# A fused FFT, feed-forward and expert kernel: plain float32 forward products for the first batch, steps moved from GpSimd to VectorE, and another order at the opening, the join and the last block

## The chip, the cores and the metric

The kernel runs on one core of one Trainium2 chip. The metric is the device time of one execution in microseconds (us), taken as the median of several runs. The engines are TensorE (PE in the profile, with its weight loads as PEld), VectorE (DVE), ScalarE (ACT), GpSimd (POOL) and SyncE (SP, which issues most of the transfers).

## The reference

Three stages follow one another over 8 batches of 3072 tokens with 256 channels (24,576 tokens). All that matters of it:

```python
y = irfft(rfft(x, axis=1) * (filt_r + 1j * filt_i), n=3072, axis=1)
h = y @ w_in                                     # 256 -> 2048
y = where(h > 0, h, exp(min(h, 0)) - 1) @ w_out  # 2048 -> 256
e = argmax(y @ w_gate); p = softmax(y @ w_gate)[e]
out = p * sigmoid(y @ w_output_gate)[e] * (relu(y @ w1[e]) @ w2[e])   # 8 experts, 256 -> 1024 -> 256
```

`w_in` and `w_out` arrive as float64. All else is float32.

## The kernel before, in words

**Products.** A float32 value is split into a high part, which is a fast float32r number, and a low part; a product of two values is three float32r products (high by high, high by low, low by high). A table that is known beforehand comes already split from memory.

**The Fourier stage.** One batch has two halves of 128 channels, and a unit of work is one half. A unit first runs butterflies on VectorE (`f1`, `f2`, lines 174 to 196 with the helper of line 167). Then six pairs of frequency groups follow, each with these steps: `hi` (ACT, line 235) and `lo` (DVE, line 239) split the input, `neg` (ACT, line 245) makes the negative, `fwd` multiplies by the forward table on PE (length 128, line 264: six float32r products of 128x256 for a group; the two real groups use plain float32, line 260), `mul` and `add` (DVE, lines 281 to 294) apply the filter, `yhi` and `ylo` (lines 299, 303) split again, `inv` (PE, lines 317 and 318) multiplies by the inverse table, and `evac` (ACT, line 332) empties PSUM. Backward butterflies in parts called `q0`, `q1`, `q2` and so on (lines 377 to 416, 465 to 470) produce `y`.

**The opening.** Before the list of slots starts, both units of batch 0 run in one stream (`us[0]`, `us[1]`). Their filter and table tiles lie in room that the weights use later (`own`). Two of the second unit's first butterflies (lines 174, 175) run on GpSimd (`pool=(0, 1)`). Into the same stream go the first steps of `Wide`, which turns a quarter of the float64 weights into float32 halves: `load`, `scale` (ACT), `bits` and `value` (DVE, lines 557, 558, 561), `high` (ACT, line 564) and `low` (GpSimd, line 568), and for `w_out` also `turn` and `gate_w` (lines 948 to 960), which multiply by the gate weights. The framework's scheduler orders the opening on each engine. It ends with the first 512 tokens' `ys`, split on ACT (line 1111) and DVE (line 1113).

**Slots.** Everything up to the end of the feed-forward stage is a list of slots. Slot (c, m) is one sixteenth of a chunk of 512 tokens: `mm1` (six products of 128x512, line 685), the elu (ACT lines 689 and 690, DVE line 691), the split of the result (line 697 on ACT, 698 on DVE), and, three slots later, `mm2` (twelve products of 128x264, line 708). There are 48 chunks, so 768 slots. `at(slot, fn, pe)` hangs further steps on a slot, `level` spreads a list of DVE steps over a stretch of slots by a table of load (`LOAD`, n/960 + 0.155 for a step of n columns), `plan_unit` lays a Fourier unit of a later batch over the slots from `t0` with `GAP` slots between pairs, and `plan_rest` places what the opening leaves over: the other quarters of the weights, the rest of batch 0's backward steps (`q2` on GpSimd), and small loads. Within a slot the order on every engine is the order of the code.

**The join and the expert stage.** While the last chunks run, the tokens are sorted by expert (`rank`, `scatter`). Two early blocks of 256 tokens (numbers -2 and -1) are computed at the seam: `transposes` (line 1286), `up2` (48 products, line 1334) and `down` (48 products, line 1349), then the table of blocks is read and `blocks(0, 98)` runs over the others; a block's rows come by `load_rows` (line 1278), and `put` (line 1363, GpSimd) scatters each half of its output, as two halves `q`. A block takes the transposes of the next one between its own `up2` and `down`. Behind the blocks stands a test of how many more there are (the load is at line 1447); here the branch isn't taken.

Of the kernel before, what the change touches and what calls it, by code (L numbers as in the profile page):

```python
# [56 lines left out]
def dft_tables():  # L57
# [7 lines left out]
    fwd, inv = [], []  # L65
    for a, b in PAIRS:
        for g in (a, b):
            kap = KAPPA[g]
            if kap is None:
# [6 lines left out]
                fwd.append(np.concatenate([ca, cb, sa, sb], 1).astype(np.float32))  # L76
                rr, ii = np.zeros((W, 2 * W)), np.zeros((W, 2 * W))
# [5 lines left out]
            else:  # L83
# [7 lines left out]
    return np.concatenate(fwd, 1).astype(np.float32), np.concatenate(inv, 1).astype(np.float32)  # L91
# [3 lines left out]
class Fft:  # L95
# [35 lines left out]
    def unit(self, b, h, own=None):  # L131
# [397 lines left out]
class Wide:  # L529
# [9 lines left out]
    def steps(self, src, place, place_c, dst):  # L539
# [34 lines left out]
def fft_moe_kernel(ctx, tc, x, filt_r, filt_i, w_in, w_out, wg, wog, w1, w2, out):  # L574
# [3 lines left out]
    fwd_np, inv_np = dft_tables()  # L578
# [901 lines left out]
```

## Time and profile before

| what | us |
|---|---|
| runs shown | 3808.22, 3808.24, 3805.9 |
| median | 3808.22 |
| the profiled execution's own time | 3805.89 |
| its span in the profile | 3804.1 |
| PE busy in the span | 3700.6 (97%) |
| DVE / ACT / POOL busy | 2537.9 / 2067.4 / 625.6 |
| granted clock of PE over the span | 0.990 |

The span is what the profile shows of the execution; the profiled execution's time lies 1.8 us above it and 2.3 us below the median. The span falls into four parts: the opening up to the first slot at 118.4 us, the slots up to about 2600 us, the join up to about 2634 us, and the blocks up to 3789 us. The granted clock is a share of full speed, 2.4 GHz; 0.5 is 1.2 GHz.

### The profile page before, as it was taken

The numbers are of one execution on the slowest core, as the hardware profiler recorded it, in microseconds if no ns is written. First come the engines' busy times: TensorE is split into PE (matmuls) and PEld (weight loads), VectorE is DVE, ScalarE is ACT, GpSimd is POOL, SyncE is SP. The second block draws the span as 40 slices with busy tenths as digits, with TensorE's granted clock in tenths as the row PEclk, the third lists the DMA queues.
The fourth block names the chain that finished last, engine by engine and source line by source line (L and its number), as shares of the span: only waits on it lengthen the run. The fifth ranks groups of instructions, "written<-read, shape, count | busy, mean of one in ns | idle before, by whom it ended". The sixth has DMA issues, their size and how long they took to land. (4 is left out here: it accounts for less than half of the span.)

```text
span 3804.1 us, 70253 instructions
## 1 busy us (share of the span) xinstructions
PE 3700.6 (97%) x26364; PEld 3481.6 (92%) x26364; DVE 2537.9 (67%) x5210; ACT 2067.4 (54%) x3897; POOL 625.6 (16%) x730
## 2 busy tenths in 40 slices
PE   4799999999999999999999999999999999999998
PEld 4689899999999999999999999999999999999998
DVE  8889888888888788788887875554333333333333
ACT  3466666666666666666666666664333333333332
POOL 1311111111111111111111111111111111111111
PEclk9799999999999999999999999999999999999999
DMA  7354434343353442533425232201212121222221
GB/s 220 120 161 142 131 124 138 103 157 111 106 158 111 133 127 86 172 114 124 137 96 160 95 109 70 91 18 41 90 47 93 46 91 46 91 91 69 68 91 38
DMA packets 235411, 400.83 MB, mean 105 GB/s; under 512 B 21554, under 2 KB 154298, under 8 KB 228922
## 3 DMA queue, kind: packets, MB, share of 16 engines
q1 hardware_dynamic: 216250, 344.68, 29.1%
q0 software_dynamic: 18816, 51.60, 3.7%
q8 instruction: 210, 3.44, 0.4%
q14 instruction: 135, 1.11, 0.1%
HBM read 674.76 MB, written 115.04 MB: 208 GB/s over the span
## 5 line engine op out<-in xcount | busy, mean ns | idle before, releaser
L708 PEld LDWEIGHTS z<-wex,g 128*128 128x128 f32 x9216 | 1229.4, 189 | 71.0 <-DVE rt L726 3.4
L708 PE MATMUL z<-wex,g 128*128 128x264 f32 x9216 | 1251.4, 285 | 3.0 <-DVE rt L726 3.0
L685 PE MATMUL h<-ys,win 128*128 128x512 f32 x4608 | 1206.6, 397 | 23.0 <-DVE e L691 11.4
L685 PEld LDWEIGHTS h<-ys,win 128*128 128x128 f32 x4608 | 818.0, 189 | 163.5 <-DVE e L691 14.3
L691 DVE SCALAR_TENSOR_TENSOR e<-e,h 128x512 f32<-128x512 f32 x768 | 525.7, 685 | 477.7 <-ACT e L690 469.5
L689 ACT ACTIVATE e<-h 128x512 f32<-128x512 f32 x768 | 459.4, 598 | 682.3 <-PE h L685 670.6
L1334 PE MATMUL h<-zt,w1s 128*128 128x256 f32 x4800 | 592.1, 283 | 1.0 <-ACT zt L1288 0.7
L1334 PEld LDWEIGHTS h<-zt,w1s 128*128 128x128 f32 x4800 | 581.9, 191 | 1.9 <-ACT zt L1288 0.9
L1349 PE MATMUL o<-w2s,hs 128*128 128x256 f32 x4704 | 573.6, 281 | 0.0
L1349 PEld LDWEIGHTS o<-w2s,hs 128*128 128x128 f32 x4704 | 556.1, 188 | 0.1
L698 DVE TENSOR_TENSOR g<-e,g 128x512 fp32r<-128x512 f32 x768 | 548.1, 714 | 0.1
L690 ACT ACTIVATE e<-e 128x512 f32<-128x512 f32 x768 | 485.8, 633 | 24.5
L1340 DVE SCALAR_TENSOR_TENSOR hs<-h,hs 128x512 fp32r<-128x512 f32 x392 | 271.2, 692 | 306.1 <-ACT hs L1339 302.4
L697 ACT CAST g<-e 128x512 fp32r<-128x512 f32 x768 | 464.3, 605 | 6.7 <-DVE e L691 6.7
L1339 ACT ACTIVATE hs<-h 128x512 fp32r<-128x512 f32 x392 | 234.1, 597 | 330.9 <-PE h L1334 329.2
L1363 POOL DMA_INDIRECT out_dram<-o,rows x196 | 192.8, 984 | 964.7 <-ACT o L1356 547.5
L779 POOL DMA_INDIRECT rows_d<-rt,sl x192 | 206.7, 1076 | 779.6 <-DVE sl L775 345.2
L1356 ACT ACTIVATE o<-o,ogv 128x256 f32<-128x256 f32 x196 | 82.2, 470 | 452.6 <-PE o L1349 452.6
L1300 DVE TENSOR_SCALAR ogv<-ogv 128x2 f32<-128x2 f32 x98 | 16.6, 169 | 376.0 <-ACT ogv L1299 376.0
L756 POOL TENSOR_TENSOR A<-A,ohb 128x8 bf16<-128x8 bf16 x192 | 69.1, 360 | 911.7 <-DVE rt L747 846.3
L803 POOL TENSOR_TENSOR ps<-pw,ps 128x512 fp32r<-128x512 f32 x64 | 88.2, 1378 | 365.4 <-ACT ps L798 347.4
L317 PE MATMUL pf<-ci,YH 128*128 128x256 f32 x528 | 129.9, 282 | 1.5 <-ACT YH L299 1.5
(288 smaller groups left out, 2882.8 us busy)
## 6 DMA issues: line engine op xcount, KB each, us to landing
w1s<-wpk SPq DMA_DIRECT2D x198, 1024.0 KB
w2s<-wpk SPq DMA_DIRECT2D x198, 1024.0 KB
ci<-dft_inv SPq DMA_DIRECT2D x73, 768.0 KB
cf<-dft_fwd SPq DMA_DIRECT2D x87, 512.0 KB
wpk<-ps SPq DMA_DIRECT2D x64, 512.0 KB
rows<-rows_d SPq DMA_DIRECT2D x98, 258.0 KB
y<-yd SPq DMA_DIRECT2D x46, 512.0 KB
fl<-fs SPq DMA_DIRECT2D x84, 256.0 KB
```

The lines of the kernel that those rows point to most:

```text
L685: nc.tensor.matmul(out=ps, lhsT=win_s(m // 4)[:, a, k, m % 4 * W:m % 4 * W + W], rhs=s[:, q, k], start=(n == 0), stop=(n == 5))
L689: nc.scalar.activation(out=e, in_=ps, func=AF.Relu, scale=-1.0)
L690: nc.scalar.activation(out=e, in_=e, func=AF.Exp, scale=-1.0)
L691: v.scalar_tensor_tensor(out=e, in0=e, scalar=-1.0, in1=ps, op0=ALU.add, op1=ALU.max)
L697: nc.scalar.copy(out=s[:, 0], in_=e)
L698: v.tensor_tensor(out=s[:, 1], in0=e, in1=s[:, 0].bitcast(F32), op=ALU.subtract)
L708: nc.tensor.matmul(out=Z[c][i], lhsT=s[:, q, i * W:i * W + W], rhs=wex_s(m // 4)[:, a, m % 4], start=(m == 0 and q == 0 and a == 0), stop= ...
L779: g.indirect_dma_start(out=rows_d, out_offset=bass.IndirectOffsetOnAxis(ap=f["sl"][:, i:i + 1], axis=0), in_=f["rt"][:, i, NE:NE + ROW], i ...
L1334: nc.tensor.matmul(out=ps[:, q * TB:q * TB + TB], lhsT=w1s(mp // 2)[:, a, k, m * W:m * W + W], rhs=s[:, z, k], start=(n == 0), stop=(n == 5))
L1339: nc.scalar.activation(out=hi, in_=p2, func=AF.Relu)
L1340: v.scalar_tensor_tensor(out=lo, in0=p2, scalar=0.0, in1=hi.bitcast(F32), op0=ALU.max, op1=ALU.subtract)
L1349: nc.tensor.matmul(out=pss[q], lhsT=hs(z, k // 2)[:, k % 2, q * W:q * W + W], rhs=w2s(k // 4)[:, a, k % 4], start=(k == 0 and n == 0), sto ...
```

## The change

1. **Forward products of batch 0.** The groups of length 128 are multiplied as two plain float32 products (of 128x256) by an unsplit table (`plain`, 512 or 768 columns in place of 1024). `lo` does nothing there and `neg` covers one half of what it did.
2. **From GpSimd to VectorE.** `low` of `Wide` (eight in all), the two first butterflies of the second unit, and the `q2` steps of batch 0 run on VectorE.
3. **Less ahead of the first slot.** Of the second quarter of `w_in` and the second of `w_out`, only `scale` and a load stand there; the first quarter of `w_out` is converted between the two halves' last steps (up to `gate_w`), its remaining steps behind them. `low` of a quarter of `w_out` is a step of its own behind the second `gate_w`.
4. **Slots.** `plan_rest` has another table with its loads counted; the two units of batch 1 start at slots 30 and 58 in place of 20 and 56, the first with three slots between pairs in place of four; the load of its input moves from slot 8 to 13.
5. **Join.** The transposes of the two early blocks go four and three slots ahead of where `up2(-2)` starts (before: three ahead, and two behind). The rows of block 0 are loaded ahead of the weights; its transposes stand inside `down(-1)`, behind 36 of its 48 products. The load for the later test moves ahead of the blocks.
6. **Last block.** `down` computes all of output half 0, then all of half 1.

The core of the diff:

```diff
+                plain.append(fwd[-1])
...
+                plain.append(np.concatenate([c, s], 1).astype(np.float32))
...
-            H = P[i]["H"] = st.tile([W, 2, 2, 3, W], F32R, tag="H", name="H", bufs=2)
+            H = P[i]["H"] = st.tile([W, 2, 2, 3, W], F32 if own else F32R, tag="H", name="H", bufs=2)
             for dst, src in halves(i, H):
                 nc.scalar.copy(out=dst[:, 0], in_=src)
...
         def lo(i):
+            if own:
+                return
...
-                nc.scalar.activation(out=H[:, :, j, 2], in_=H[:, :, j, 0].bitcast(F32), func=AF.Copy, scale=-1.0)
+                parts = slice(0, 1) if own else slice(0, 2)
+                nc.scalar.activation(out=H[:, parts, j, 2], in_=H[:, parts, j, 0].bitcast(F32), func=AF.Copy, scale=-1.0)
...
-                cc = p["c"][:, 512 * j:512 * j + 512]
+                cc = p["c"][:, 256 * j:] if own else p["c"][:, 512 * j:512 * j + 512]
...
+                if own:
+                    for m in range(2):
+                        nc.tensor.matmul(out=o, lhsT=cc[:, m * W:m * W + W],
+                                         rhs=p["H"][:, 0, j, m:m + 2].rearrange("p c d -> p (c d)"), start=(m == 0), stop=(m == 1))
...
         def low():
             hi, lo = dst()
-            nc.gpsimd.tensor_tensor(out=lo, in0=T["c"], in1=hi.bitcast(F32), op=ALU.subtract)
+            v.tensor_tensor(out=lo, in0=T["c"], in1=hi.bitcast(F32), op=ALU.subtract)
...
-            LOAD[t] = {2: 0.85, 3: 1.65, 6: 1.4, 12: 0.7, 13: 0.7}.get(t % 16, 0.0)
+            LOAD[t] = {14: 0.7, 15: 0.7}.get(t, 0.0) if t < 16 else {2: 0.85, 3: 1.65, 6: 1.4, 12: 0.7, 13: 0.7}.get(t % 16, 0.0)
...
-    GAP = 4
-
-    def plan_unit(b, h, t0, prev, nxt, early=False):
+
+    def plan_unit(b, h, t0, GAP, prev, nxt, early=False):
...
-            level([(213, fn) for fn in p["q2"]] + [(1024, fn) for fn in p["y2"][:2]] + [(0, p["y2"][2])], t1 + 5, t1 + 16)
+            level([(213, fn) for fn in p["q2"]] + [(1024, fn) for fn in p["y2"][:2]] + [(0, p["y2"][2])], t1 + 5, t1 + 12)
...
-        return steps + [lambda: turn(0), lambda: gate_w(0), lambda: turn(1), lambda: (low(), gate_w(1))]
+        return steps + [lambda: turn(0), lambda: gate_w(0), lambda: turn(1), lambda: gate_w(1), low]
...
-        c = cf[i] = fft.st.tile([W, 1024], F32R, tag="cf", name="cf") if ORDER.index(i) % 2 else room("win1")[:, 0:1024]
-        nc.sync.dma_start(out=c.bitcast(F32), in_=fwd_d[:, 1024 * i:1024 * i + 1024])
+        c = fft.st.tile([W, 1024], F32, tag="cf", name="cf") if ORDER.index(i) % 2 else room("win1", F32)[:, 0:1024]
+        o, n = sum(768 if k == 2 else 512 for k in range(i)), 768 if i == 2 else 512
+        cf[i] = c[:, 0:n]
+        nc.sync.dma_start(out=cf[i], in_=plain_d[:, o:o + n])
...
-          fft.unit(0, 1, dict(own, AT=X00.rearrange("p a k d -> p (a k) d"), Z=Z1, T=Z1, pool=(0, 1)))]
-    parts = [u["parts"](nc.gpsimd) for u in us]
+          fft.unit(0, 1, dict(own, AT=X00.rearrange("p a k d -> p (a k) d"), Z=Z1, T=Z1, pool=()))]
+    parts = [u["parts"](v) for u in us]
...
-    for fn in wide_steps[1, 0][1:] + wide_steps[0, 1][1:] + wide_steps[1, 1][:1]:
+    for fn in (wide_steps[0, 1][1], wide_steps[1, 0][1]):
         fn()
...
+        if h == 0:
+            for fn in wide_steps[1, 0][2:8]:
+                fn()
...
+    for fn in wide_steps[1, 0][8:] + wide_steps[1, 1][:1]:
+        fn()
     Y[0] = ys0
-    U0 = 11
+    U0 = 18
...
+        for k, q, slots, tg in ((0, 1, (None, None, 0, 1, 2, 2), ()),
+                                (1, 1, (None, 2, 3, 3, 4, 5), (4, 5, 5, 6)),
+                                (0, 2, (3, 5, 6, 6, 7, 7), ()),
+                                (1, 2, (4, 6, 7, 7, 8, 9), (8, 9, 9, 10)),
+                                (0, 3, (7, 9, 10, 10, 11, 12), ()),
+                                (1, 3, (8, 10, 11, 11, 12, 13), (12, 13, 13, 14))):
+            st = wide_steps[k, q]
...
-    def down(j, then=lambda k: None):
+    def down(j, then=lambda k: None, last=False):
...
+        for k, q in [(k, q) for q in range(2) for k in range(8)] if last else [(k, q) for k in range(8) for q in range(2)]:
+            for n, (z, a) in enumerate(((0, 0), (0, 1), (1, 0))):
+                nc.tensor.matmul(out=pss[q], lhsT=hs(z, k // 2)[:, k % 2, q * W:q * W + W], rhs=w2s(k // 4)[:, a, k % 4],
+                                 start=(k == 0 and n == 0), stop=(k == 7 and n == 2))
+            if q:
+                then(k)
+            if k < 7:
+                continue
...
-            down(j, then=lambda k: load_w(j + 1, 1, k // 4) if more and k % 4 == 3 else None)
+            down(j, then=lambda k: load_w(j + 1, 1, k // 4) if more and k % 4 == 3 else None, last=not more)
...
+                t0 = (U0 + 12, U0 + 40)[h] if b == 1 else 96 * (b - 1) - 4 + 48 * h
+                gap = 3 if (b, h) == (1, 0) else 4
...
-                          (-3, lambda: transposes(-2), True), (-2, lambda: gates(-2), False),
+                          (-4, lambda: transposes(-2), True), (-3, lambda: transposes(-1), True), (-2, lambda: gates(-2), False),
                           (0, lambda: up2(-2, (0, 1)), True), (1, table_count, True), (1, lambda: up2(-2, (2, 3)), True),
-                          (2, lambda: transposes(-1), True), (2, lambda: down(-2), True),
+                          (2, lambda: down(-2), True),
...
+        es_m2.close()
+        es_m.close()
+        open_moe2()
+        load_rows(0)
...
+        def beside(k):
+            if k == 5:
+                transposes(0)
+            if k % 4 == 3:
+                load_w(0, 1, k // 4)
+
+        down(-1, then=beside)
...
+        some_more = nc.values_load(T2["nblk"], engines=[mybir.EngineType.SP, mybir.EngineType.PE, mybir.EngineType.DVE, mybir.EngineType.Activation, mybir.EngineType.Pool], min_val=0, max_val=NBLK, skip_runtime_bounds_check_because=why)
         blocks(0, NBLK - 3 - NEARLY)
-    some_more = nc.values_load(T2["nblk"], engines=[mybir.EngineType.SP, mybir.EngineType.PE, mybir.EngineType.DVE, mybir.EngineType.Activation, mybir.EngineType.Pool], min_val=0, max_val=NBLK, skip_runtime_bounds_check_because=why)
```

How the change moves instructions shows at three places. First, GpSimd's own list from its start (each row is a line, operation and names; the numbers in names only tell tiles apart). Before:

```order
L174 TENSOR_TENSOR Z<-win_120 128x1024
L175 TENSOR_TENSOR win_120<-win_120 128x1024
L568 TENSOR_TENSOR win_658<-win_120,win_658 128x1024
L568 TENSOR_TENSOR wex_811<-raw,wex_811 128x4x256
L568 TENSOR_TENSOR win_846<-raw,win_846 128x1024
L405 TENSOR_TENSOR Z_118<-Z_118 128x128
```

After (line 765 is the 754 of before, in the slots):

```order
L765 COPY A_1511<-acc_79 128x8
L767 ISA
L767 TENSOR_TENSOR A_1511<-A_1511,ohb 128x8 x4
L790 DMA rows_d<-rt,sl 196608x258 x2
L814 TENSOR_TENSOR ps<-pw,ps 128x512
```

The two butterflies, every `low` and the `q2` steps have left GpSimd's list.

Second, VectorE at the end of the opening, from the last steps of the last pairs on (`raw` is the weights' raw tile, `Z` the backward butterflies). Before:

```order
L303 TENSOR_TENSOR YH<-ab,YH 128x512
L557 TENSOR_SCALAR raw<-raw 128x1024
L303 TENSOR_TENSOR YH<-ab,YH 128x512
L558 SCALAR_TENSOR_TENSOR raw<-raw 128x1024
L557 TENSOR_SCALAR raw<-raw 128x1024
L561 SCALAR_TENSOR_TENSOR raw<-raw 128x1024
L558 SCALAR_TENSOR_TENSOR raw<-raw 128x1024
L377 TENSOR_TENSOR Z_118<-Z_118 128x768
L561 SCALAR_TENSOR_TENSOR raw<-raw 128x1024
L960 TENSOR_TENSOR wex_811<-pf,wex_811 128x2x8 x2
```

After:

```order
L313 TENSOR_TENSOR YH<-ab,YH 128x512
L415 TENSOR_TENSOR AA<-Z_118 128x128
L416 TENSOR_TENSOR AA<-Z_118 128x128
L567 TENSOR_SCALAR raw<-raw 128x1024
L313 TENSOR_TENSOR YH<-ab,YH 128x512
L568 SCALAR_TENSOR_TENSOR raw<-raw 128x1024
L387 TENSOR_TENSOR Z_118<-Z_118 128x768
L571 SCALAR_TENSOR_TENSOR raw<-raw 128x1024
```

Of two groups of three weight steps one is left there.

Third, PE at the join (`er` are the early blocks' rows, `zt` their transposed halves, `z` the last slots' `mm2`). Before, from the last `mm2` to `down(-2)`:

```order
L708 MATMUL z_28463<-wex_948,g 128x264
L708 MATMUL z_28465<-wex_948,g 128x264
L1334 MATMUL h_28898<-zt,w1s 128x256 x12
L1334 MATMUL h_28913<-zt,w1s 128x256 x12
...
L1334 MATMUL h_28941<-zt,w1s 128x256 x12
L1334 MATMUL h_28956<-zt,w1s 128x256 x12
L1286 MATMUL pf<-ct,er 128x128 x4
L1349 MATMUL o_28987<-w2s,eh 128x256 x3
```

After, from the slots ahead of it on:

```order
L1311 MATMUL pf<-ct,er 128x128 x4
L719 MATMUL z_28362<-wex_866,g 128x264 x2
L719 MATMUL z_28364<-wex_866,g 128x264 x2
...
L1311 MATMUL pf<-ct,er 128x128 x4
L719 MATMUL z_28362<-wex_866,g 128x264 x2
...
L1359 MATMUL h_28847<-zt,w1s 128x256 x12
L1359 MATMUL h_28862<-zt,w1s 128x256 x12
L1375 MATMUL o_28885<-w2s,eh 128x256 x3
```

Block -1's transposes have gone from between `up2(-2)` and `down(-2)` to between two slots' `mm2`.

## Rows read from the trace of the kernel before

**Rows 1.** The page, part 1: busy time of each engine over the whole span.
```profile
PE 3700.6 (97%) x26364; PEld 3481.6 (92%) x26364; DVE 2537.9 (67%) x5210; ACT 2067.4 (54%) x3897; POOL 625.6 (16%) x730
```

**Rows 2.** Busy time in chosen stretches; columns: stretch, length, engines (instructions), granted clock, DMA, GB/s.
```profile
31.00:97.00 66.00, 44.91 (x290) 40.93 (x291) 62.16 (x125) 33.41 (x68) 2.36 (x1) 0.87 0.71 224
97.00:118.30 21.30, 6.68 (x28) 5.11 (x26) 19.24 (x37) 5.27 (x9) 5.52 (x2) 0.56 0.37 111
118.30:206.10 87.80, 72.42 (x391) 62.38 (x391) 73.71 (x99) 49.68 (x86) 29.54 (x26) 0.87 0.36 112
...
480.00:2560.00 2080.00, 2080.00 (x13594) 1904.98 (x13593) 1630.74 (x3151) 1390.02 (x2549) 332.32 (x426) 1.00 0.36 116
```

**Rows 3.** Timeline of the opening: start, duration, engine, line, names [idle before <- releaser].
```profile
8.14 1.22 DVE L174 TENSOR_TENSOR AA<-X 128x1024 f32<-128x1024 f32 x1 [6.83 <-DMA X<-in_x_dram]
...
29.09 1.23 DVE L176 SCALAR_TENSOR_TENSOR win<-Z,win 128x1024 f32<-128x1024 f32 x1 [4.64 <-POOL win L175]
```

**Rows 4.** The same timeline at 83 us: POOL's `low` of line 568 beside DVE.
```profile
83.29 2.36 POOL L568 TENSOR_TENSOR win<-win,win 128x1024 fp32r<-128x1024 f32 x1 [54.23 <-ACT win L564]
83.52 2.68 DVE L239 TENSOR_TENSOR H<-X,H 128x512 fp32r<-128x512 f32 x1
```

**Rows 5.** The same timeline, DVE from 97 to 110 us.
```profile
97.66 1.22 DVE L561 SCALAR_TENSOR_TENSOR raw<-raw 128x1024 uint32<-128x1024 uint32 x1
98.80 1.22 DVE L558 SCALAR_TENSOR_TENSOR raw<-raw 128x1024 uint32<-128x1024 uint32 x1
...
100.80 3.39 DVE L561 SCALAR_TENSOR_TENSOR raw<-raw 128x1024 uint32<-128x1024 uint32 x1
...
107.17 0.42 DVE L407 TENSOR_TENSOR AA<-AA,Z 128x256 f32<-128x256 f32 x1
107.50 2.56 DVE L408 TENSOR_TENSOR AA<-AA,Z 128x256 f32<-128x256 f32 x1
```

**Rows 6.** The same timeline, PE: forward products of the opening, float32r (L264) and plain (L260).
```profile
33.50 1.32 PE L264 MATMUL zf<-H,cf 128*128 128x256 f32 x6
...
52.58 1.06 PE L260 MATMUL zf<-X,cf 128*128 128x128 f32 x8
...
74.13 1.24 PE L264 MATMUL zf<-H,win 128*128 128x256 f32 x9
```

**Rows 7.** The timeline of PE: first products of slots 0, 17 and 18.
```profile
118.37 6.39 PE L685 MATMUL h<-ys,win 128*128 128x512 f32 x17 [4.12 <-DVE ys L1113]
...
195.48 1.57 PE L685 MATMUL h<-ys,win 128*128 128x512 f32 x6
...
198.33 1.56 PE L685 MATMUL h<-ys,win 128*128 128x512 f32 x6
```

**Rows 8.** The timeline of PE at the join, with SP's row of the loads of rows.
```profile
2611.49 1.04 PE L1286 MATMUL pf<-ct,er 128*128 128x128 f32 x4 [2.09 <-DVE ex L772]
2612.19 4.58 PE L1349 MATMUL o<-w2s,eh 128*128 128x256 f32 x26
...
2625.94 3.28 PE L1349 MATMUL o<-w2s,eh 128*128 128x256 f32 x26
...
2627.04 1.27 SPq L1278 DMA_DIRECT2D rows<-rows_d  x2
...
2631.70 0.60 PE L1286 MATMUL pf<-ct,rows 128*128 128x128 f32 x4
2632.97 0.38 PE L1334 MATMUL h<-zt,w1s 128*128 128x256 f32 x1 [0.68 <-ACT zt L1288]
2633.70 5.89 PE L1334 MATMUL h<-zt,w1s 128*128 128x256 f32 x47 [0.34 <-DVE zt L1289]
```

**Rows 9.** The timeline of all engines at the end.
```profile
3783.57 5.76 PE L1349 MATMUL o<-w2s,hs 128*128 128x256 f32 x48
...
3789.03 0.84 ACT L1356 ACTIVATE o<-o,ogv 128x256 f32<-128x256 f32 x2 [4.65 <-PE o L1349]
3789.78 0.98 POOL L1363 DMA_INDIRECT out_dram<-o,rows  x1 [6.19 <-ACT o L1356]
3792.97 0.98 POOL L1363 DMA_INDIRECT out_dram<-o,rows  x1 [2.21 <-DMA out_dram<-o,rows]
```

More of the change, by code (lines that the diff above doesn't have):

```diff
@@ L64, in dft_tables @@
     p = np.arange(64)
-    fwd, inv = [], []
+    fwd, inv, plain = [], [], []
     for a, b in PAIRS:
@@ L88, in dft_tables @@
                 fwd.append(np.concatenate([chi, clo, shi, slo], 1))
+                plain.append(np.concatenate([c, s], 1).astype(np.float32))
                 m = np.concatenate([-s.T, c.T, s.T], 1) * (2.0 / S)
                 inv.append(np.concatenate(_split(m), 1))
-    return np.concatenate(fwd, 1).astype(np.float32), np.concatenate(inv, 1).astype(np.float32)
+    return tuple(np.concatenate(t, 1).astype(np.float32) for t in (fwd, inv, plain))
 class Fft:
@@ L577, in fft_moe_kernel @@
     SP = mybir.EngineType.SP
-    fwd_np, inv_np = dft_tables()
+    fwd_np, inv_np, plain_np = dft_tables()
+    plain_d = nc.inline_tensor(plain_np, name="dft_plain").ap()
     fwd_d = nc.inline_tensor(fwd_np, name="dft_fwd").ap()
@@ L877, in level @@
             LOAD[t] += k
-    UPAIR = [("ldf", 0), ("hi", 0), ("lo", 1), ("neg", 2), ("fwd", 2), ("mul", 3), ("ldk", 4), ("add", 4), ("yhi", 5),
+    UPAIR = [("ldf", 0), ("hi", 0), ("lo", 1), ("neg", 2), ("fwd", 2), ("mul", 3), ("ldk", None), ("add", 4), ("yhi", 5),
              ("ylo", 6), ("inv", 7), ("evac", 8)]
-    GAP = 4
-    def plan_unit(b, h, t0, prev, nxt, early=False):
+    def plan_unit(b, h, t0, GAP, prev, nxt, early=False):
         u = fft.unit(b, h)
+        pair = [(nm, 8 - GAP if nm == "ldk" else d) for nm, d in UPAIR]
         for n, i in enumerate(ORDER):
-            for nm, d in UPAIR:
+            for nm, d in pair:
                 t = t0 + GAP * n + d
@@ L900, in plan_unit @@
         else:
-            free = prev + GAP * 5 + 2
-            level(f1[:6], prev + 7, free - 1)
+            free = prev[0] + prev[1] * 5 + 2
+            level(f1[:6], prev[0] + 7, free - 1)
             level(f1[6:] + f2, free, t0 - 1)
-        for t in range(t0, t0 + 33):
-            for nm, d in sorted(UPAIR, key=lambda q: -q[1]):
+        for t in range(t0, t0 + 5 * GAP + 9):
+            for nm, d in sorted(pair, key=lambda q: -q[1]):
                 for n, i in enumerate(ORDER):
@@ L929, in plan_unit @@
         level(q0, t0 + 13, t1 - 1)
+        if b == 1:
+            level(q1 + y2, t1, t0 + 35)
+            return
         level(q1, t1, t0 + 41)
@@ new lines, in plan_rest @@
+        for k, q, slots, tg in ((0, 1, (None, None, 0, 1, 2, 2), ()),
[5 rows of a table added]
+            st = wide_steps[k, q]
+            for fn, t, n in zip(st[:5] + st[-1:], slots, (0, 0, 1700, 1024, 0, 1024)):
+                if t is not None:
+                    at(t, fn)
+                    if n:
+                        LOAD[t] = load_of(t) + weight(n)
+            for fn, t in zip(st[5:9], tg):
+                at(t, fn, True)
+        for h, y1, q2 in ((0, (1, 2), (4, 11)), (1, (2, 4), (12, 19))):
+            p = parts[h]
+            level([(1024, p["y1"][0]), (512, p["y1"][1])], *y1)
+            level([(384, fn) for fn in p["m"]] + [(213, fn) for fn in p["q2"]] + [(1024, fn) for fn in p["y2"][:2]]
+                  + [(0, p["y2"][2])], *q2)
@@ L1134, in plan_rest @@
         for e in range(NE):
-            at(1 + e, lambda e=e: pads(e))
+            at(3 + e, lambda e=e: pads(e))
         for e in range(1, NEARLY):
-            at(9, lambda e=e: pads(0, e * TB))
-        at(10, lambda: (es_s.close(), open_moe1_rest()))
-        at(8, lambda: fft.load(1, 0))
-        at(12, og_ld)
-        at(15, og_turn, True)
-        at(17, og_st)
+            at(11, lambda e=e: pads(0, e * TB))
+        at(12, lambda: (es_s.close(), open_moe1_rest()))
+        at(13, lambda: fft.load(1, 0))
@@ L1144, in load_half @@
+        at(14, og_ld)
+        at(16, og_turn, True)
+        at(18, og_st)
     def load_half(c, h):
@@ L1341, in up2 @@
             then(mp)
-    def down(j, then=lambda k: None):
+    def down(j, then=lambda k: None, last=False):
         hs = HS.pop(j)
         pss = [pz.tile([W, D], F32, tag=f"z{q}", name="o2") for q in range(2)]
-        for k in range(8):
-            for q in range(2):
-                for n, (z, a) in enumerate(((0, 0), (0, 1), (1, 0))):
-                    nc.tensor.matmul(out=pss[q], lhsT=hs(z, k // 2)[:, k % 2, q * W:q * W + W], rhs=w2s(k // 4)[:, a, k % 4],
-                                     start=(k == 0 and n == 0), stop=(k == 7 and n == 2))
-            then(k)
         t, sc = R.pop(j), SC.pop(j)
         ZT.pop(j)
-        for q in range(2):
+        for k, q in [(k, q) for q in range(2) for k in range(8)] if last else [(k, q) for k in range(8) for q in range(2)]:
[5 more added lines that the diff above has]
+            if k < 7:
+                continue
             o = T2["o", j][:, q] if j < 0 else P2["r"].tile([W, D], F32, tag=f"o{q}", name=f"o{q}")
@@ L1374, in blocks @@
                 load_rows(j)
-        transposes(j0)
+            transposes(j0)
         for j in range(j0, j1):
@@ L1436, in fft_moe_kernel @@
             load_w(0, 0, h)
-        es_m2.close()
-        es_m.close()
-        open_moe2()
-        for j in range(3):
+        for j in range(1, 3):
             load_rows(j)
-        down(-1, then=lambda k: load_w(0, 1, k // 4) if k % 4 == 3 else None)
+        def beside(k):
[4 more added lines that the diff above has]
+        down(-1, then=beside)
         for j in range(-NEARLY, 0):
```

21 lines of the change are left out of this document (3 added, 18 removed).

## The prediction

> **What bounds the kernel now.** I read the page first, then the busy time by stretches, then the timeline where PE pauses. PE is busy for 3700.6 us of the span [rows 1], so 103.5 us in all are pauses. From 480 to 2560 us there is none: 2080 of 2080 us [rows 2]. What another order can win lies in the first 200 us, at the join and at the end.
>
> In the opening VectorE sets the pace: from 31 to 97 us it is busy for 62.2 of 66.0 us, PE for 44.9; from 97 to 118.3 us for 19.2 of 21.3, PE for 6.7 at a granted clock of 0.56 [rows 2]. From 118.3 to 206.1 us PE is busy for 72.4 of 87.8 us, the clock 0.87, and VectorE for 73.7: nobody is full, the two wait for each other in turn.
>
> **The opening, to the first slot.** VectorE's first butterfly starts at 8.14 us [rows 3] and slot 0 goes on in earnest at 118.37 [rows 7]: 110.2 us. What must VectorE issue in it? Starts 1.14 us apart for 1024 columns and 0.33 for 256 [rows 5] give columns/960 + 0.067 us for one instruction. By that the 175 instructions of its list up to the first half's `ys` sum to 92.3 us. Of the other 17.9 us, 4.6 are the wait for GpSimd's butterfly [rows 3]. Further 6.3 are three instructions that ran long while GpSimd did `low` or just as it did: 2.68 us [rows 4] for a size that the formula puts at 0.60 from start to start and 0.68 in length, so 2.0 too many; 3.39 in place of 1.22, 2.2 too many; 2.56 in place of 0.42, 2.1 too many [rows 5]. Some 7.0 are left for waits on ACT and PE along the chain of a pair.
>
> After the change the list to the same point has 163 instructions. Gone are 14 `lo` (eight of 512 columns, six of 256: 8 x 0.60 + 6 x 0.33 = 6.8) and one group of three weight steps (0.6 + 2 x 1.13 = 2.9); added are two butterflies (2.3) and one `low` (1.1). That makes 86.0, or 6.3 less. GpSimd's list has nothing left in the opening, so the 4.6 and the 6.3 go too. The 7.0 stay: `hi`, `fwd`, `mul` still follow one another. So slot 0 comes at 8.1 + 86.0 + 7.0 = 101.1, which is **17.2 us** earlier. Ends: 10 (below) and 21, if half of the 7.0 goes with `lo`.
>
> *The plain products.* There are 22 groups (132 products of line 264 before, six each). A float32r product of 256 columns takes 0.12 us at full clock ((1.24 - 0.28)/8, with 0.28 the length of the last) and 0.21 at the low level ((1.32 - 0.28)/5) [rows 6]: 0.72 us a group. The trace has plain products of 128 columns only: four, recorded as eight, in 1.06 us, 0.265 each [rows 6]. For 256 columns the price lies between 0.24 (two records at the float32r rate) and 0.53 (twice 0.265). I take 0.53, the same type's own row. A group then takes 1.06 us, and PE does 22 x 0.34 = 7.5 us more. I cost that at nothing: VectorE covers it, with PE busy for only 44.9 of 66 us. Without that cover the gain would be 17.2 - 7.5 = 9.7: the lower end.
>
> The Trainium skill, "FP8 and Floating Point Precision", section "TensorE Precision Notes", speaks against this edit: true float32 makes four passes through the array. By that two products are eight passes where six stood, 22 x 0.24 = 5.3 us more on PE; the double record of each plain product in the trace is half of it at most, and no run here shows the passes themselves. The sum would be the same, since either price is covered; in the first rival, where the cover is gone, it gives 3784 in place of 3786.
>
> Half-sized tables, the half-sized `neg` and ACT's smaller share (33.4 of 66.0 us busy, DMA share 0.71) [rows 2] cost and gain nothing: VectorE's list covers them.
>
> **Slots 0 to 17.** They took from 118.37 to 198.33 [rows 7], 80.0 us. In three groups of six slots VectorE's list comes to 19.3, 19.9 and 23.3 us by the formula, and 20.2 for PE in the second: the longer ones sum to 62.8. So 17.2 are waits and long instructions. After the change VectorE has 22.4, 23.5 and 15.9: `low` and `q2` are added, and the Fourier unit of batch 1 starts ten slots later. In the last six PE is the longer: six slots at 2.85 apart [rows 7] are 17.1, and I allow 3.4 for transposes and gate products, 20.5. Sum 66.4. Between none of the 17.2 staying and all of it the stage takes 66.4 to 83.6. I take the middle, 75.0, since GpSimd's part in the waits ends while ACT's chain (line 690 before 691) stays: **5.0 us** less, between 13.6 less and 3.6 more.
>
> **Slots 18 to 95.** What was pushed back is done here: VectorE's list grows from 212.5 to 227.6 us. PE has 78 slots at 2.85, 222.3, and some 300 Fourier and small products by 0.12, 36: 258 in all. Taking the longer of the two for every three slots, PE pauses 4.3 us before and 4.2 after, nearly all from slot 84 on. I cost it at **nothing** (0 to 4 more): PE's own work covers it, and where that cover ends is rival 3.
>
> **Join.** Block -1's transposes stood 2.09 us idle ahead of them, and `down(-2)` then began at a low clock: 26 products in 4.58 us, where `down(-1)` takes 3.28. Block 0's `up2` waited 0.68 and 0.34 behind its transposes [rows 8]. That is 4.4 us. With transposes among the `mm2`, PE has other work meanwhile. The moved test's load comes onto every queue here; I allow 0.4: **4.0 us** less. What could be late next: block 0's transposes inside `down(-1)` queue 12 of its products and all of `up2(0)` behind them. They stand behind 36 products (36 x 0.12 = 4.3 us). Their rows landed within 4.7 us before, since the transposes at 2631.70 waited for nothing and the load was issued at 2627.04 [rows 8]. They go out earlier now, ahead of two weight loads, which they delay in SP's queue. Lower end 2.0.
>
> **Last block.** The 48 products take 5.76 us; ACT empties both halves behind them, and the second `put` waits 2.21 us for the first to land [rows 9]. With half 0 done 24 x 0.12 = 2.88 us sooner, its `put` goes at about 3786.9 and the second at 3789.8 in place of 3792.97: **3.2 us** less (2.0 to 3.5).
>
> **Sum.** -17.2 - 5.0 - 4.0 - 3.2 = -29.4. On the profiled execution of 3805.9 that makes 3776.5. The median stands 2.3 above that execution, so I predict **3779** for the median. All good ends together give -21 - 13.6 - 4.4 - 3.5 = -42.5 (3766), all bad ones -9.7 + 3.6 + 4 - 2 - 2 = -6.1 (3802).
>
> **Rivals.** (1) *PE's plain products decide the opening.* If ACT and VectorE wait for each forward stage, the 7.5 us land on the path: -21.9, so **3786**. For it: at half clock a group would take twice its 1.06 us, and the clock was 0.56 late in the opening [rows 2]. Against it: from 31 to 97 us PE is free for a third of the time. Chance 0.15.
> (2) *The waits on GpSimd only change their name.* VectorE gets its 6.3 us, but then stands where it stood for the inputs of the next step, loads or ACT, and the 10.9 come back: -18.5, so **3790**. For it: nobody was full from 118 us on. Against it: loads use 0.71 of the queues' time and `low` on VectorE needs nothing late. Chance 0.10.
> (3) *VectorE never catches up: slower.* One mechanism: the 15.1 us pushed into slots 18 to 95 keep it behind PE, so the regime of 118 to 206 us, with each waiting for the other at a granted clock of 0.87 [rows 2], lasts until slot 95. The 258 us of PE work then take 258 x (1/0.87 - 1) = 38.6 us more, and the 5.0 don't come: -29.4 + 5.0 + 38.6 = +14.2, so **3822**. It decides where VectorE's list is longer than PE's over many slots. For it: 227.6 of 258 leaves 12%, and before it was 18%. Against it: up to slot 83 PE's sum is the larger in every six slots, and before, the same kind of slots kept PE full from 480 us on [rows 2]. Chance 0.07.
> (4) *The change doesn't do what it says:* the opening is held by loads, slots give back what it gains, and only join and end pay: -7.2, about 3801. Chance 0.06.
>
> **How the numbers follow.** The forecast, 3768 to 3788, has 0.62. The range of 3765 to 3795 holds it with rivals 1 and 2 and leaves out 3 and 4 and some of the tails. About 0.2%, 7.6 us, is what a measurement of this kernel tells from no change: faster, below 3800.6, has 0.87; the same 0.06; slower 0.07.
>
> **What would show it.** Slot 0's products near 101 us, no pause of VectorE behind GpSimd and no instruction of 256 to 1024 columns over 2 us ahead of it; two plain products a group between 0.24 and 0.53 us each; slots 0 to 17 in 66 to 84 us; no idle of over 1 us ahead of `down(-2)` and `up2(0)`; the last `put` issued within 1.5 us of PE's last product. Wrong if: PE waits for VectorE's elu (line 691) beyond slot 30, slot 0 comes later than 108 us, or PE pauses inside `down(-1)`.

## The result, and the profile after

The changed kernel took 3775.3 us (median of four, 3773.42 to 3777.2), the kernel before 3808.23 beside it: a ratio of 0.9915, interval 0.9899 to 0.9930. So it is 32.9 us faster; 3779 was predicted, with 3765 to 3795 as the range. The profiled execution has a span of 3773.6 us, 30.5 below that of before.

The page, part 1, after:

```profile
PE 3698.4 (98%) x26320; PEld 3477.6 (92%) x26320; DVE 2530.5 (67%) x5226; ACT 2063.6 (55%) x3897; POOL 584.1 (15%) x700
```

PE's work is the same within 2.2 us [rows 1]; its pauses shrank from 103.5 us to 75.2. Busy time by stretches, after (columns as in [rows 2]):

```profile
31.00:80.00 49.00, 36.13 (x182) 31.39 (x181) 44.08 (x93) 26.16 (x57) 0.00 (x0) 0.82 0.82 269
80.00:100.45 20.45, 12.87 (x77) 10.73 (x78) 20.45 (x49) 8.08 (x15) 0.00 (x0) 0.83 0.08 28
100.45:173.24 72.79, 62.21 (x363) 54.05 (x364) 65.20 (x103) 45.57 (x77) 0.22 (x1) 0.91 0.49 156
173.24:260.00 86.76, 86.49 (x563) 78.44 (x562) 78.91 (x149) 58.22 (x111) 17.53 (x19) 1.00 0.48 151
```

GpSimd does nothing from 31 us to slot 0 and 0.22 us in the first 18 slots. VectorE is full from 80 us to slot 0, and busy for 90% up to slot 18; from there PE is full, as before it was only from about slot 20 on.

The timeline of PE after, which answers to [rows 6] and [rows 7]: a late table, plain products at full clock and what follows them, slot 0, the longest pause in the slots, slot 18.

```profile
54.20 6.24 PE L270 MATMUL zf<-H,win 128*128 128x256 f32 x16 [3.25 <-DMA win<-dft_plain]
60.28 3.62 PE L270 MATMUL zf<-H,cf 128*128 128x256 f32 x16
...
64.69 1.89 PE L270 MATMUL zf<-H,win 128*128 128x256 f32 x8
66.23 0.47 PE L327 MATMUL pf<-ci,YH 128*128 128x256 f32 x1
...
100.45 4.30 PE L696 MATMUL h<-ys,win 128*128 128x512 f32 x11 [1.54 <-DVE ys L1132]
...
151.65 2.07 PE L696 MATMUL h<-ys,win 128*128 128x512 f32 x4 [4.93 <-DVE win L578]
...
173.24 1.56 PE L696 MATMUL h<-ys,win 128*128 128x512 f32 x6
```

Two records are one plain product. Eight records take 1.89 us and sixteen 3.62, so eight more, which are four products, cost 3.62 - 1.89 = 1.73 us: **0.43 us** for a plain product, 0.86 for a group, against 0.72 for six float32r products [rows 6]. The granted clock is 1.00 in both rows. (The next product starts 1.54 us behind the first, ahead of the last record's end: it is recorded with 0.47 us in place of 0.28, so 1.54 is less than four products cost.) At the low level (granted clock 0.50 from 40.03 to 43.60) four took 3.57.

VectorE's wait for the forward stage whose table came late:

```profile
57.99 0.69 DVE L291 TENSOR_TENSOR ab<-zf,wex 128x512 f32<-128x512 f32 x1 [2.25 <-PE zf L270]
```

The join, PE and SP after, answering to [rows 8]:

```profile
2577.54 3.04 PE L1359 MATMUL h<-zt,w1s 128*128 128x256 f32 x24
...
2584.38 3.28 PE L1375 MATMUL o<-w2s,eh 128*128 128x256 f32 x26
...
2602.73 0.66 PE L1311 MATMUL pf<-ct,rows 128*128 128x128 f32 x4 [1.42 <-DMA rows<-rows_d]
...
2604.66 6.03 PE L1359 MATMUL h<-zt,w1s 128*128 128x256 f32 x48
2610.52 0.60 PE L1311 MATMUL pf<-ct,rows 128*128 128x128 f32 x4
```

The end, after, answering to [rows 9]:

```profile
3754.89 5.76 PE L1375 MATMUL o<-w2s,hs 128*128 128x256 f32 x48
3757.89 0.48 ACT L1382 ACTIVATE o<-o,ogv 128x256 f32<-128x256 f32 x1 [2.20 <-PE o L1375]
3758.64 0.98 POOL L1389 DMA_INDIRECT out_dram<-o,rows  x1 [4.72 <-ACT o L1382]
...
3762.40 0.98 POOL L1389 DMA_INDIRECT out_dram<-o,rows  x1 [2.77 <-DMA out_dram<-o,rows]
```

And two rows of the kernel before that are needed for the sum (the first product of `up2(-2)`, and block 1's transposes):

```profile
2602.39 3.04 PE L1334 MATMUL h<-zt,w1s 128*128 128x256 f32 x24
...
2639.43 0.60 PE L1286 MATMUL pf<-ct,rows 128*128 128x128 f32 x4
```

Stage by stage, in us:

| stage | before | after | change | predicted |
|---|---|---|---|---|
| start to slot 0 | 118.37 | 100.45 | -17.9 | -17.2 |
| slots 0 to 17 | 79.96 | 72.79 | -7.2 | -5.0 |
| slot 18 to `up2(-2)` | 2404.06 | 2404.30 | +0.2 | 0 |
| `up2(-2)` to block 1's transposes | 37.04 | 32.98 | -4.1 | -4.0 |
| from there to the last `down` | 1144.14 | 1144.37 | +0.2 | 0 |
| last `down` to the end | 20.53 | 18.71 | -1.8 | -3.2 |

The sum is -30.5. Four transposes (0.36 us) that left the join stand in the slots now.

### The profile page after: what moved, and what is told of

It is laid out like the page before. It is cut to its first block, busy times and chain, and to the rows that moved or that the text cites. A ratio compares the mean times of both kernels' runs of the same rounds, so it can differ in the third digit from the quotient of the medians.

```text
span 3773.6 us, 70119 instructions
## 1 busy us (share of the span) xinstructions
PE 3698.4 (98%) x26320; PEld 3477.6 (92%) x26320; DVE 2530.5 (67%) x5226; ACT 2063.6 (55%) x3897; POOL 584.1 (15%) x700
## 5 line engine op out<-in xcount | busy, mean ns | idle before, releaser
L709 DVE TENSOR_TENSOR g<-e,g 128x512 fp32r<-128x512 f32 x768 | 539.3, 702 | 0.0
```

The costliest lines, as they stand in the source:

```text
L709: v.tensor_tensor(out=s[:, 1], in0=e, in1=s[:, 0].bitcast(F32), op=ALU.subtract)
```

## The experiments

All are the changed kernel with one edit, run beside the kernel before (its medians were 3806.7, 3806.65 and 3808.46). Slot 0 and slot 18 are the starts of their products in the trace. The opening itself varies: three profiled executions with the same opening (the changed kernel, e8 and e11) have slot 0 at 100.45, 97.79 and 97.55. So a shift of slot 0 by less than 3 us in one trace shows nothing; the times of several runs count for more. They too have a limit: the kernel before had medians between 3806.65 and 3808.46 us in these series and 3808.23 beside the changed kernel. Taken against the kernel before of its own series, each cost of e1 to e8 is 1.5 us larger than the differences given below, that of e9 0.2 smaller, and the gains of e10 to e12 are 0.2 larger; a difference of less than 2 us between runs of different series shows nothing. The series are e1 to e4, e5 to e8, and e9 to e12.

| run | median (lowest to highest) | slot 0 | slots 0 to 17 |
|---|---|---|---|
| changed kernel | 3775.3 (3773.42 to 3777.2) | 100.45 | 72.8 |
| e1, six float32r products | 3787.97 (3786.5 to 3789.28) | 111.59 | 73.6 |
| e2, two butterflies on GpSimd | 3779.99 (3779.04 to 3782.59) | 103.51 | 72.9 |
| e3, `low` on GpSimd | 3778.64 (3777.0 to 3781.09) | 101.99 | 73.2 |
| e4, plain products twice | 3788.61 (3787.43 to 3791.27) | 110.58 | 72.6 |
| e5, all back on GpSimd | 3779.6 (3779.39 to 3782.23) | 105.03 | 72.9 |
| e6, a `lo` that nobody reads | 3782.05 (3781.85 to 3782.62) | 107.21 | 73.0 |
| e7, wide tables | 3776.53 (3776.24 to 3779.49) | 101.93 | 72.7 |
| e8, join and last block as before | 3779.59 (3777.1 to 3782.07) | 97.79 | 73.0 |
| e9, `lo`'s place in the chain | 3783.62 (3782.89 to 3786.28) | 108.32 | 72.8 |
| e10, tables side by side | 3771.52 (3770.63 to 3772.02) | 95.62 | 72.9 |
| e11, earlier conversions | 3773.84 (3770.55 to 3776.01) | 97.55 | 71.2 |
| e12, e10 and e11 together | 3768.05 (3767.06 to 3771.56) | 98.31 | 69.9 |

**e1: six float32r products again.** The `own` branches of `hi`, `lo`, `neg` and `fwd` are taken out, and the wide tables are back:

```diff
-            if own:
-                return
...
-                cc = p["c"][:, 256 * j:] if own else p["c"][:, 512 * j:512 * j + 512]
+                cc = p["c"][:, 512 * j:512 * j + 512]
...
-                if own:
+                if False:
```

> The changed kernel with the opening's forward products as six float32r products again, with lo, the whole neg and the wide tables. Theory A (VectorE's list sets the opening, PE's products are covered): the 14 lo put 6.8 us back on VectorE, so slot 0 goes on at 106 to 108 us in place of 100.45 and the time is 3780 to 3784. Theory B (the plain products lie on the path, lo lay beside other work): slot 0 at 98 to 101.5 us, time 3772 to 3776.

Slot 0 went on at 111.59, the time rose by 12.7 us: more than either theory gave. Theory A is right in kind, but `lo`'s 6.8 us are half of it. VectorE's two longest waits in e1's opening, behind the one for the input, and PE at the join:

```profile
DVE ab L289 <- PE zf L272: 4.2, 2, 2.3
DVE YH L311 <- ACT YH L307: 3.8, 3, 1.7
```

```profile
2615.05 1.00 PE L1307 MATMUL pf<-ct,rows 128*128 128x128 f32 x4 [2.12 <-DMA rows<-rows_d]
```

So some of e1's time may not belong to the opening at all: in this execution `up2(-2)` to block 1's transposes took 35.10 us, where it was 32.98 with the same order in the changed kernel. Block 0's transposes waited for their rows for 2.12 us in place of 1.42, and the granted clock behind that wait was 0.52.

**e6 and e9: what else is in e1?** e6 computes `lo` where no product reads it. e9 puts an instruction of the same size and number into the chain ahead of the products, without a change of value:

```diff
             for dst, src in halves(i, P[i]["H"]):
+                if own:
+                    tt(out=dst[:, 0], in0=src, in1=dst[:, 0], op=ALU.max)
+                    continue
```

> The changed kernel with lo computed in the opening again, though no product reads it: VectorE's 14 instructions alone, 6.8 us. Theory A (lo's own time and, beyond it, its place in the chain from hi to fwd each cost): slot 0 goes on at 106.5 to 108 us, time 3780 to 3784; the other 4.3 us of the run with six products belong to the chain. Theory B (all of that run's 11.1 us are VectorE's and the scheduler's order with lo in it): slot 0 at 110 to 112, time 3786 to 3789. Theory C (lo lies beside waits): slot 0 at 100 to 103.

> The changed kernel with the 14 instructions at the place of lo again, but now in the chain: each takes the larger of the input and its copy (the same value) into the part that the plain products and neg read, so a pair goes hi, VectorE, neg and fwd. Theory A (lo's place in the chain makes the last 4.3 us of the run with six products): slot 0 goes on at 110 to 112.5 us, time 3785 to 3789. Theory B (those 4.3 us belong to the six products, their tables or the larger neg): slot 0 at 105 to 108.5, as with the lo that nobody reads, time 3780 to 3783.5.

The timeline of PE, slot 0 of e6, and below it of e9:

```profile
107.21 6.23 PE L694 MATMUL h<-ys,win 128*128 128x512 f32 x17 [1.90 <-DVE ys L1130]
```

```profile
108.32 4.36 PE L697 MATMUL h<-ys,win 128*128 128x512 f32 x11 [1.65 <-DVE ys L1133]
```

e6 costs 6.8 us of time, what 14 instructions take in VectorE's list (theory A, by the time and by slot 0): for what stands in VectorE's list, the opening is VectorE's. e9 costs 8.3; the 1.5 between them are no more than two series differ by, so it isn't shown that the place in the chain costs anything. Its time (3783.62) lies 4.4 below e1's. By slot 0 theory B of e9 holds: what is left belongs to the six products, their tables, the larger `neg` or, for some 2 us of e1's trace, the join.

**e7: the tables' size.** A second load fills each table's tile up to 1024 columns:

```diff
+        nc.sync.dma_start(out=c[:, n:1024], in_=plain_d[:, o:o + 1024 - n])
```

> The changed kernel with a second load behind each forward table of the opening that brings its tile to 1024 columns again; no product reads what it loads. Theory A (loads of the opening are covered): slot 0 at 100 to 101.5 us, time 3773 to 3777. Theory B (the half-sized tables are part of the gain): slot 0 2 to 4 us later, time 3777 to 3780.

1.2 us slower at 101.93, less than the spread of the opening and than what two series differ by: theory A holds by the time, and a cost of up to 3 us isn't excluded. How the rest of e1 divides between the products, `neg`, the tables and the join stays open.

**e4: is PE covered in the opening?** Every pair of plain products is issued twice:

```diff
-                    for m in range(2):
+                    for m in (0, 1, 0, 1):
```

> The changed kernel with every pair of plain products of the opening issued twice: PE does 22 x 0.77 = 17 us more. Theory A (VectorE covers PE in the opening): slot 0 at most 4 us later (by 104.5), time 3775 to 3780. Theory B (the forward stage is on the path of each pair): slot 0 later by 8 to 17 us, time 3783 to 3793.

22 x 0.86 = 19 us more on PE (the expectation's 17 took a group at 0.77) gave 13.3 us of time, slot 0 at 110.58. Theory A falls. The groups of VectorE's waits up to slot 0 in e4:

```profile
DVE YH L313 <- ACT YH L309: 3.1, 4, 1.4
DVE ys L1132 <- ACT ys L1127: 2.0, 1, 2.0
DVE raw L567 <- DMA raw<-in_moe_w_out_dram: 1.6, 1, 1.6
DVE fb L291 <- PE zf L265: 1.3, 1, 1.3
DVE ab L291 <- PE zf L270: 0.9, 2, 0.5
```

No single wait is long. Not all of the 13.3 us is a lack of cover, though. The scheduler that orders the opening put 2.9 us of weight steps more ahead of the second half's `ys` in VectorE's list. And only 10.1 us of it lie ahead of slot 0; at the join this execution took 34.39 us in place of 32.98, with a wait of 2.83 us for block 0's rows. So of the 19 us on PE some 7 to 10 came through in the opening (its own spread is 3 us), and the rest was covered.

**e2, e3, e5: GpSimd.** The two butterflies; `low`; both with `q2`:

```diff
-          fft.unit(0, 1, dict(own, AT=X00.rearrange("p a k d -> p (a k) d"), Z=Z1, T=Z1, pool=()))]
-    parts = [u["parts"](v) for u in us]
+          fft.unit(0, 1, dict(own, AT=X00.rearrange("p a k d -> p (a k) d"), Z=Z1, T=Z1, pool=(0, 1)))]
+    parts = [u["parts"](nc.gpsimd) for u in us]
...
-            v.tensor_tensor(out=lo, in0=T["c"], in1=hi.bitcast(F32), op=ALU.subtract)
+            nc.gpsimd.tensor_tensor(out=lo, in0=T["c"], in1=hi.bitcast(F32), op=ALU.subtract)
```

> The changed kernel with the second unit's two butterflies on GpSimd again. Theory A (VectorE stood behind GpSimd): VectorE issues 2.3 us less and waits some 4.6 us for GpSimd, so slot 0 goes on 2 to 3 us later, at 102.5 to 103.5, time 3777 to 3779. Theory B (the wait only changes its name, as what comes next isn't ready either): slot 0 at 98 to 101 us, time 3773 to 3776.

> The changed kernel with all eight low on GpSimd again and nothing else. Theory A (an instruction of VectorE beside low runs some 2 us longer): 1.1 us less and 2.1 us more for each low, one or two of them ahead of slot 0 (101 to 102.5 us), six in the slots, some 3 to 8 us in all: time 3778 to 3784. Theory B (low on GpSimd costs VectorE nothing): 9 us come off VectorE in stretches where it is full: time 3766 to 3771.

> The changed kernel with low, the two butterflies and the backward steps q2 of batch 0 on GpSimd, as before; the plain products stay. Theory A (the edits add up): 3.1 us from the butterflies and 1.5 from low, slot 0 goes on at 104.5 to 106 us, time 3780 to 3785. Theory B (the price worked out before, 10.9 us less the 3.4 of moved work): slot 0 at 107.5 to 109, time 3783 to 3788.

The waits of VectorE in e5, up to slot 0:

```profile
DVE ab L291 <- PE zf L270: 4.8, 1, 4.8
DVE win L178 <- POOL win L177: 4.6, 1, 4.6
```

The wait of 4.6 us is back to the tenth [rows 3]. e2 costs 4.7 us and lies just beyond theory A; e3 costs 3.3, inside its theory A; but both and `q2` together cost only 4.3: they don't add up in the time, while slot 0 in e5 lies at 105.03, inside theory A. In the slots there is nothing: 72.9 us with `low` and `q2` on GpSimd, 72.8 without.

**e8: the join and the last block as before.**

```diff
-                          (-4, lambda: transposes(-2), True), (-3, lambda: transposes(-1), True), (-2, lambda: gates(-2), False),
+                          (-3, lambda: transposes(-2), True), (-2, lambda: gates(-2), False),
...
-                          (2, lambda: down(-2), True),
+                          (2, lambda: transposes(-1), True), (2, lambda: down(-2), True),
...
-            if k == 5:
-                transposes(0)
...
-            down(j, then=lambda k: load_w(j + 1, 1, k // 4) if more and k % 4 == 3 else None, last=not more)
+            down(j, then=lambda k: load_w(j + 1, 1, k // 4) if more and k % 4 == 3 else None)
```

> The changed kernel with the join and the last block as before. Theory A (both gains are real and independent): from up2(-2) to the transposes of block 1 37 us in place of 33, the last put 1.9 us later against the last down; time 3780 to 3783. Theory B (the join's pauses are filled by what comes behind them anyway): at most 2 us in all, time 3775 to 3777.5.

PE at the join in e8:

```profile
2574.62 3.04 PE L1359 MATMUL h<-zt,w1s 128*128 128x256 f32 x24
...
2583.73 0.63 PE L1311 MATMUL pf<-ct,er 128*128 128x128 f32 x4 [2.09 <-DVE ex L783]
2584.11 3.36 PE L1375 MATMUL o<-w2s,eh 128*128 128x256 f32 x26
...
2603.68 0.38 PE L1359 MATMUL h<-zt,w1s 128*128 128x256 f32 x1 [0.67 <-ACT zt L1313]
2604.41 5.89 PE L1359 MATMUL h<-zt,w1s 128*128 128x256 f32 x47 [0.34 <-DVE zt L1314]
2610.14 0.60 PE L1311 MATMUL pf<-ct,rows 128*128 128x128 f32 x4
```

All the idle times of before are there (2.09, 0.67, 0.34), but in this execution not the low clock: 26 products took 3.36 us behind the same 2.09 us of idle that had 4.58 behind it before [rows 8]. From `up2(-2)` to block 1's transposes it is 35.52 us, not 37. So the order is worth 35.52 - 32.98 - 0.36 (the transposes that left) = 2.2 us at the join, and 1.9 at the end (the last `put` 9.40 us behind the last `down`'s start, 7.51 with the change); together 4.1, and the time says 4.3. Theory A's direction holds; its size at the join does not. The end is the surer half. At the join the same stretch took 32.71 to 35.10 us in the twelve profiled executions with the new order, so one execution with the old order at 35.52 gives the size only roughly; and e8's runs fall into two pairs (3777.1 and 3777.32, 3781.85 and 3782.07), of which the trace shows one of the faster.

**e10, e11, e12: what was left.** After the change two pauses stand out: VectorE's 2.25 us for a forward stage whose table came late (PE's 3.25 at 54.20), and PE's 4.93 for `low` at slot 12. e10 lets four of the half-sized tables lie side by side (`win1c` is the whole room) and loads them early. e11 moves conversions:

```diff
-        c = fft.st.tile([W, 1024], F32, tag="cf", name="cf") if ORDER.index(i) % 2 else room("win1", F32)[:, 0:1024]
+        c = fft.st.tile([W, 1024], F32, tag="cf", name="cf") if i in (2, 5) else win1c[:, (0, 512, 1024, 1536)[(0, 1, 3, 4).index(i)]:]
...
-    for i in (1, 3, 4, 5):
-        f_load(i)
+    f_load(1)
+    ld_c(1)
+    f_load(3)
+    ld_c(3)
+    f_load(4)
+    ld_c(4)
+    f_load(5)
...
-                                (0, 2, (3, 5, 6, 6, 7, 7), ()),
+                                (0, 2, (2, 4, 5, 5, 6, 6), ()),
...
-                                (0, 3, (7, 9, 10, 10, 11, 12), ()),
-                                (1, 3, (8, 10, 11, 11, 12, 13), (12, 13, 13, 14))):
+                                (0, 3, (6, 8, 9, 9, 10, 10), ()),
+                                (1, 3, (8, 11, 12, 12, 13, 14), (13, 14, 14, 14))):
```

> The changed kernel with four of the six half-sized tables side by side in the one room that held two in turn, so that their loads are issued from the start, between the filter's. Theory A (PE's wait of 3.3 us for a table at 54 us is what VectorE waits for with 2.2 us): slot 0 goes on 1.5 to 4 us earlier, at 96 to 99 us, time 3771.5 to 3774. Theory B (the filter's loads are then late instead): slot 0 at 99.5 to 103 us, time 3775 to 3779.

> The changed kernel with the third and fourth quarter of w_in converted one or two slots earlier and the fourth of w_out one later. Theory A (PE's 4.9 us of wait for low at slot 12 is an order of steps on VectorE, which has time behind it): slots 0 to 17 in 67.5 to 70 us in place of 72.8, time 3771 to 3773.5. Theory B (VectorE is full up to there, so the wait moves to other slots): 72 to 74 us, time 3774 to 3777.

> The tables side by side and the earlier conversions together. Theory A for both, adding up: slot 0 at 96 to 99 us, slots 0 to 17 in 67.5 to 70 us, time 3767.5 to 3771.5. Theory B: time 3773 to 3778.

e10 follows theory A: VectorE waits for no forward stage any more, and the time is 3.8 us lower, outside the changed kernel's spread. e11 is inconclusive by its time (its runs lie across those of the changed kernel) and lands between the theories in its trace. PE's timeline in e11:

```profile
142.81 1.66 PE L696 MATMUL h<-ys,win 128*128 128x512 f32 x6 [0.44 <-DVE e L702]
...
153.14 1.06 PE L969 MATMUL pf<-wg_sb,ts 128*128 128x8 f32 x8 [0.46 <-ACT ts L964]
...
155.37 1.88 PE L969 MATMUL pf<-wg_sb,ts 128*128 128x8 f32 x8 [0.68 <-ACT ts L964]
157.10 2.91 PE L696 MATMUL h<-ys,win 128*128 128x512 f32 x6
```

The pause at slot 12 is gone (0.44 in place of 4.93), but slots 12 to 17 still took 26.0 us in place of 27.3: around two sets of gate products and the waits ahead of them the granted clock was 0.67 (from 153 to 159.8 us), and six products took 2.91 us where 1.56 is usual. In e12 the same slots took 24.7, slots 0 to 17 69.9 and the time is 3.5 below e10's, so theory A of e12 holds; three of its four runs are faster than every run of e10. e12 is the fastest version: 3768.05 us, ratio 0.9895 to the kernel before (0.9880 to 0.9911), and its slowest run is faster than the fastest of the changed kernel.

## Why the prediction was right, and where it was not

**The opening.** The sum held (-17.9 for -17.2); its parts did not. *"By that the 175 instructions ... sum to 92.3 us"* and 86.0 after: the list as a price is borne out by e6, where 6.8 us of list cost 6.8 us of time. (The edits that the prediction names leave 161 instructions, not 163; the time of 86.0 follows from them.) But GpSimd's part was priced at 10.9 us, 7.5 net of the 3.4 us of moved work, and undoing it costs 4.3, or 5.9 by its own series (e5): too high by 2 to 3. The plain products' part was priced as `lo` alone, 6.8, and undoing it costs 12.7 (e1), of which some 2 may be the join: too low by 4 to 6. That the sum held is in part luck, as the two errors cancel.

The step that failed is *"The 7.0 stay: `hi`, `fwd`, `mul` still follow one another"*. VectorE's waits in the opening, without the one for the input, were 4.6 us after (2.6 and 2.1 in e8 and e11, with the same opening) and 9.4 in e1. So with six products and `lo` the chain waits more. That some of GpSimd's wait would then only have changed its name, as rival 2 said, and that the plain products took it away, fits these numbers but was not tested by itself.

**"I cost that at nothing: VectorE covers it"** is too strong as a mechanism. e4 shows that of 19 us of added PE work some 7 to 10 come through in the opening. It did little harm because the product was mis-sized in the other direction: 0.43 us, where 0.53 was taken, so a group costs 0.14 more than before and not 0.34, 3.1 us in all and not 7.5. The 0.53 is twice 1.06/4, and the 1.06 holds the last record's 0.28, which the same paragraph takes off for float32r. Taken off here too, [rows 6] give (1.06 - 0.28)/7 = 0.111 a record, 0.22 for a product of 128 columns and 0.45 for one of 256. (The row for the "low level" has a granted clock of 1.00; e1's join, at 0.52, has the same 0.21 us for a float32r product, so the value stands.) Rival 1 has the right mechanism in part, but its 7.5 us could not come, as PE had only 3.1 more to do. By the Trainium skill ("FP8 and Floating Point Precision", section "TensorE Precision Notes") true float32 makes four passes; by that 4 x 0.12 = 0.48 us is the estimate for such a product, and the trace has 0.43, 3.6 float32r products of the same size.

**Slots 0 to 17.** 72.8 us, 75.0 predicted. The reason given, *"since GpSimd's part in the waits ends"*, is not the one: with `low` and `q2` on GpSimd the stage takes 72.9 (e5). What is left is the plan (the later unit, weight steps ahead of or behind slot 0); no run undid it, so that is argued, not shown. VectorE is busy for 65.2 of the 72.8 us, and one misplaced `low` held PE for 4.9.

**Slots 18 to 95.** Nothing was predicted and nothing came (+0.2): VectorE is busy for 241.8 us of these 78 slots, 234.6 before, and that lies beside PE's work. Rival 3, with the regime of a clock of 0.87 up to slot 95, is out: from slot 18 to 260 us the clock is 1.00 and PE has 86.49 of 86.76 us, and up to slot 95 it is 0.99 with PE busy for 263.6 of 267.8.

**The join.** -4.1 for -4.0, but 1.3 of the 4.4 us that were added up was the low clock in `down(-2)`, which the trace of e8 with the old order doesn't show. That the transposes would find their rows was the weak step, and named as such: PE waited 1.42 us inside `down(-1)`. The bound of 4.7 us ran from the load's issue; but the load itself waits in SP's queue (3.2 us) for the last scatter to land. SP's wait there, GpSimd and SP, after:

```profile
SPq L1303 <- DMA rows_d<-rt,sl: 3.2, 1, 3.2
...
2596.81 0.97 POOL L790 DMA_INDIRECT rows_d<-rt,sl  x1 [2.35 <-ACT eh L1364]
...
2599.47 0.40 SPq L1303 DMA_DIRECT2D rows<-rows_d  x1
```

The last scatter goes 19.3 us behind the start of `up2(-2)`, and `down(-1)` now starts just then (2596.84), so its 36 products of cover end before the rows are there. This wait is not a fixed 1.42 us: it was 2.12 in e1 and 2.83 in e4.

**The last block.** -1.8 for -3.2, just outside the range of 2.0 to 3.5. The second `put` was to go when ACT is done; it waits for the first to land, as before (2.77 us, 2.21 before [rows 9]). So only the first `put`'s head start of 2.5 us is won, less the 0.6 that the wait grew by.

The median came 3.7 us below the forecast; the two terms that were too small (slots, opening: 2.9) and the one that was too large (end: 1.4) make 1.5 of it, the rest is how the profiled executions lie to their medians (2.3 below the median before, at it after).

**The signs of being wrong.** Two of the three came true: PE paused inside `down(-1)`, and it waited 2.42 us for VectorE's elu at slot 91 (line 702 now). The second was ill chosen, since before the change PE waited for the elu at slots 88 to 91 too, 2.7 us in all. The last `put` was issued 1.75 us behind PE's last product, not within 1.5.

**What isn't shown.** Undoing the plain products, GpSimd's part and the two ends costs 12.7, 4.3 and 4.3 us, 21.3 of the 32.9 (26.0 by their own series). The rest is put down to what no run undid by itself: the weight steps that left the opening (2.9 us by the list) and the plan of the slots.

## What to carry to other kernels

Where one engine's list sets a stage, the sum of its instructions is a good price for what is added or taken away, but the other engines of the chain are not free beside it: test the cover by doubling their work before it is costed at nothing. Price an instruction by the steps between the starts of a row's own records: the row's length holds the last one's tail. Where several waits run in turn, their removal need not be additive, so undo each part alone and all together. A stretch that is shortened should be looked at again for the next late input; here two such places gave a further 7 us.

## What the runs showed of the hardware

A plain float32 product of 128x256 takes 0.43 us at full clock, one of 128x128 0.22 [rows 6], so the price goes with the columns. The same 2.09 us of idle ahead of `down(-2)` was followed by the low clock in one execution (before, 26 products in 4.58 us) and by the full clock in another (e8, 3.36), and inside `down(-1)` a wait of 2.12 us by the low clock (e1, granted clock 0.52) and one of 2.83 by the full (e4, 1.00). So a low stretch behind a short pause is no fixed price of it. And the same opening ended at 97.6 to 100.5 us in three executions.
